# One more tile in the ring of x, and a fill, an unread write and the end marks set apart, in a fused attention and mixture-of-experts kernel

## The chip, the cores and the metric

The kernel runs on one core of a Trainium2 chip. The metric is the device time of one execution in microseconds; the time before is the median of three runs, and one further execution was profiled.

## What is computed

The reference is channel attention followed by a routed two-layer network on its output. Shapes: q, k, v are 4 x 5056 x 256, so there are 20224 tokens of 256 numbers; 8 experts with 256 x 1024 and 1024 x 256 weights.

```python
qn = q / (np.linalg.norm(q, axis=1, keepdims=True) + 1e-06)
kn = k / (np.linalg.norm(k, axis=1, keepdims=True) + 1e-06)
s = kn.transpose(0, 2, 1) @ qn / tau
a = softmax of s over its last axis
x = (v @ a).reshape(20224, 256)

do_compute = x @ w_skip > 0
out = x.copy()
xc = x[do_compute]
logits = xc @ w_gate
e_idx = np.argmax(logits, axis=1)
gate_w = softmax(logits)[row, e_idx]
for e in range(8):
    h = np.maximum(xc[e_idx == e] @ w1[e], 0.0)
    y[e_idx == e] = gate_w[e_idx == e, None] * (h @ w2[e])
out[do_compute] = xc + y
```

## The kernel before

**Stages.** Each of the four batches is cut into four chunks of ten tiles of 128 tokens, 16 chunks in all. For a chunk c, `scores` (L743) multiplies k by q into a sum over the batch, ten steps of two fp32 matmuls, each of which the profile shows as two records. `softmax` turns a batch's sum into the matrix `aug`, split in a high and a low part for exact enough products. For a chunk d, `attend` (L816 to L818) multiplies v by it, five products of twelve matmuls, each into one of the buffers `px`. `keep_x` (L825, L826) copies a product out of `px` on ScalarE (ACT): x goes into a tile `xo` of the ring `xos`, the router's logits into `lg`. `store` (L835 to L838) writes x to `out`, and `route` finds each token's place in its expert's list and scatters the chunk's ten tiles of 128 rows with indirect DMAs from GpSimd (POOL) into `srt` (L899). After every second scatter `pace` (L650) writes zeros on POOL that nobody reads.

**Experts.** The lists of the first `D0` = 6 chunks are enough to begin: seven blocks of 512 tokens of one expert are loaded ahead (`load_ahead`: the columns `xs` by L285, the rows `xg` by L289), multiplied (`first_ahead`, `second_ahead`, L338 to L340 and L361 to L365), finished on VectorE (DVE, L371) and scattered into `out` (L236). When all lists stand, `end_lists` (L671) writes marks behind each list on POOL, four indirect DMAs from the tile `none`, so that reads past an end find no token. `no_rows` (L644) fills 1024 rows behind the last list from the same tile. After the marks come eight small tiles (`Small`, rows `yg` by L530 to L532, weights `v1r` and `v2r` by L248), between the last blocks ahead, and then a loop over large halves.

**What sets the order.** All of this up to the loop is written as tasks of a planner, `Plan`: each task has an engine (D is the queue of SyncE, SP, which issues nearly all loads and stores, in order), a cost, dependencies and a due time. `PLACES` gives due times to PE's steps: A are scores, B are products with v, H blocks ahead, S small tiles. The planner runs its tasks by their costs and writes the instructions in the order that results; on each engine that order is then fixed, and each instruction waits for what it needs. A task `t` of chunk `d` that takes a tile of the ring gets the dependencies `stored[d - NXO]` and `sorted_[d - NXO]`.

**Waits between DMAs on one tensor.** All scatters, marks and loads touch `srt`, at addresses known only at run time. Helpers name groups of accesses that need not wait for each other: `in_list` puts scatters and marks into the group "scatter"; `beside(i, group, others)` puts an instruction into `group` and frees it from those of `others`. Loads ahead are put into "first lists" and freed from "later lists", and scatters of chunks from `D0` on into "later lists" and freed from "first lists". The marks are in neither.

Of the kernel before, what the change touches and what calls it, by code (L numbers as in the profile page):

```python
# [20 lines left out]
P = 128  # L21
B = 4
N = 5056
C = 256
# [11 lines left out]
S1 = 120  # L36
# [9 lines left out]
NA = 266  # L46
JH = J // 2
NQ = 5
NXO = 3

PLACES = """
A0 -212.84 779.51, A1 1321.85 2287.98, A2 1288.02 1918.41, A3 921.83 1283.14, A4 -211.85 1066.57, A5 1.96 1135.44, A6 1521.56 1748.04, A7 866.77 2427.61, 
A8 1669.19 1909.96, A9 1529.84 1745.34, A10 49.51 1125.18, A11 964.56 1241.96, A12 76.13 775.39, A13 1533.28 1646.93, A14 284.14 322.32, A15 605.99 1645.34, 
B0 -553.38 1624.65, B1 1059.41 1229.58, B2 1324.08 2043.89, B3 774.09 2431.92, B4 187.89 1016.60, B5 1367.03 1932.84, B6 157.71 569.73, B7 202.72 464.71, 
B8 855.77 2530.12, B9 1438.10 1858.11, B10 1153.34 1832.22, B11 1096.41 1886.67, B12 777.75 2410.50, B13 798.41 1410.74, B14 1275.11 2037.27, B15 1124.02 1912.70, 
H0 756.73 1449.91, H1 1567.64 1958.30, H2 211.59 521.38, H3 380.89 734.47, H4 1225.45 2144.35, H5 297.48 436.13, H6 1041.42 1976.08, S0 1664.16 1808.51, 
S1 1589.25 1784.53, S2 1183.50 2100.39, S3 491.56 743.28, S4 317.74 323.84, S5 1044.45 2181.99, S6 1496.20 1816.03, S7 1625.43 1829.53
"""


class Plan:
# [6 lines left out]
    def add(self, engine, cost, f=None, deps=(), due=1e9, hold=None, wait=0.0):  # L68


        ways = list(zip(engine, cost)) if isinstance(cost, tuple) else [(engine, cost)]
        t = SimpleNamespace(ways=ways, engine=ways[0][0], cost=ways[0][1], f=f, deps=[d for d in deps if d], due=due, asked=None, hold=hold, wait=wait, users=None, end=None)
        self.tasks.append(t)
        return t
# [102 lines left out]
def attn_moe(ctx: ExitStack, tc: tile.TileContext, q_k, vt, tau, w_skip, w_gate, w1, w1q, w2, out):  # L177
    nc = tc.nc
# [464 lines left out]
        to = srt[E * CAP : E * CAP + 8 * P, :].rearrange("(r p) w -> p r w", p=P)  # L643
        beside(nc.sync.dma_start(to, none.rearrange("p (o w) -> p o w", o=1).to_broadcast([P, 8, RW])), "no rows", "scatter")  # L644

    idle = none[:, :C].bitcast(mybir.dt.bfloat16)

    def pace():

# [2 lines left out]
    def in_list(i):  # L652
        for g in ("scatter", "no rows"):
            tc.declare_no_dep(i.ins, group=g, reason="no place is used twice")
        tc.add_to_no_dep_group("scatter", i.ins)

    def end_lists():
        low = tab.tile([P, 1], F32, name="low")
        V.tensor_scalar(low, pidx, float(R), None, ALU.is_ge)
        ends = tab.tile([P, E // 2], F32, name="ends")  # L660
        pairs = base.rearrange("p (k h) -> p k h", h=2)
        V.tensor_tensor(ends, pairs[:, :, 1], pairs[:, :, 0], ALU.subtract)
        V.tensor_scalar(ends, ends, float(-R), None, ALU.add)
        V.scalar_tensor_tensor(ends, ends, low, pairs[:, :, 0], ALU.mult, ALU.add)
        endi = tab.tile([P, E // 2], I32, name="endi")
        V.tensor_scalar(ends, ends, pidx, None, ALU.add)
        yield
        G.tensor_copy(endi, ends)
        yield
        for k in range(E // 2):  # L670
            i = G.indirect_dma_start(  # L671
                out=srt, out_offset=IndirectOffsetOnAxis(ap=endi[:, k : k + 1], axis=0), in_=none, in_offset=None,
                bounds_check=E * CAP - 1, oob_is_err=False)
            in_list(i)
            if k % 2:
                yield

# [317 lines left out]
    for c in range(NC):  # L995
        b, ch = divmod(c, NCH)
        ld, users = {}, ([], [])
        for h in range(2):
            cuts = {(0, 0): (0, 1, 2, 3, 4, JH), (0, 1): (0, 2, JH), (1, 0): (0, 2, JH)}.get((c, h), (0, JH))
            for j0, j1 in zip(cuts, cuts[1:]):  # L1000
                t = then("qk", add("D", 0.68 * (j1 - j0), lambda c=c, h=h, j0=j0, j1=j1: load_qk(c, h, j0, j1), due=1e9 if c else -99, hold=("part", 99) if j0 else ("qk", NQ)))
                t.users = [] if j0 else users[h]
                ld.update((h * JH + j, t) for j in range(j0, j1))
        for n in range(2):
            for h in range(2):
                begins = ch == 0 and h == 0
                s0 = then(("sq", n), add("S", 1.18, lambda c=c, n=n, h=h: squares(c, n, h), [ld[j] for j in range(h * JH, (h + 1) * JH)], hold=None if begins else ("sqh", 3)))
                users[h].append(s0)
                if begins:
                    if b:  # L1010
                        s0.deps.append(ready_a[b - 1, "n"])
                    summed[n] = s0
                else:
                    summed[n] = add("V", 1.41, lambda c=c, n=n, h=h: add_squares(c, n, h), [s0, summed[n]])
                    s0.users = [summed[n]]
            if ch == NCH - 1:
                summed[n] = add("V", 1.53, lambda n=n: fold_squares(n), [summed[n]])
        g = scores(c)
        for j in range(J):
            deps = [ld[j]]  # L1020
            if j == 0 and ch == 0 and b > 1:
                deps.append(freed_s[b - 2])
            t = then("A", add("T", 0.865, lambda g=g: next(g), deps, at("A", c, j)))
            if j % JH == JH - 1:
                users[j // JH].append(t)
        last_a = t
        if c == 2:
            third = t
        if ch == NCH - 1:
            g = softmax(b)  # L1030
            s0, = chain(g, ("S", 0.5), deps=[t])
            n0, = chain(g, ("T", 0.8), deps=[s0, summed[0], summed[1]])
            s = chain(g, ("V", 0.36), ("S", 1.65), ("V", 2.3), ("V", 1.55), ("S", 2.35), ("V", 0.35), ("S", 0.75), deps=[n0])
            m0, = chain(g, ("T", 0.45), deps=s[-1:])
            m1, = chain(g, ("S", 0.5), deps=[m0])
            m2, = chain(g, ("T", 0.9), deps=[m1])
            m3, = chain(g, ("V", 0.12), deps=[m2])
            aH, = chain(g, ("S", 0.55), deps=[m3])
            aL, = chain(g, ("V", 0.65), deps=[aH])
            m0.hold = m2.hold = ("m", 1)  # L1040
            m0.users, m2.users = [m1], [m3]
            freed_s[b], ready_a[b], ready_a[b, "n"] = s0, aL, n0
            if b:
                s0.deps.append(ready_a[b - 1])
            norms_read = s[0]
# [4 lines left out]


    routed, based, stored, sorted_ = {}, {}, {}, {}
    padded = add("D", 2.6, no_rows, [third], wait=8.0)
    for d in range(NC):
        b, ch = divmod(d, NCH)
        sv = []
# [18 lines left out]
                sv[0][0].users = [t]  # L1075
        sv[1][0].users = [t]
        stored[d] = then("st", add("D", 3.4, lambda d=d: store(d), [s], at("B", d, 4, by=16.5)))
        g = route(d)
        r = chain(g, ("V", 0.43), deps=[s] + ([routed[d - 1]] if d else []))
        r += chain(g, ("S", 0.17), ("V", 1.02), ("V", 0.33), ("S", 0.18), deps=r)  # L1080
# [106 lines left out]
    t = based[NC - 1]  # L1187
# [106 lines left out]
```

## Time and profile before

| | |
|---|---|
| median of 3 runs | 754.59 us (752.77 to 755.32) |
| the profiled execution | 751.94 us |
| its span | 750.1 us, 13405 instructions |
| PE, VectorE, ACT, POOL busy | 733.9, 504.1, 351.7, 328.6 us |
| DMA over the span | 165.99 MB, mean 221 GB/s |

The span runs from the first instruction of the profile to the last; the execution's own time has about 1.8 us around it. PE stands for TensorE, DVE for VectorE. "Idle before, releaser" in a row is the time for which the engine stood before that instruction, and what ended it; a wait for several things is put down to the one that came last by the profile, and where that had long been done it was another.

### The profile page before, as it was taken

The numbers are of one execution on the slowest core, as the hardware profiler recorded it, in microseconds if no ns is written. First come the engines' busy times: TensorE is split into PE (matmuls) and PEld (weight loads), VectorE is DVE, ScalarE is ACT, GpSimd is POOL, SyncE is SP. The second block draws the span as 40 slices with busy tenths as digits, with TensorE's granted clock in tenths as the row PEclk, the third lists the DMA queues.
The fourth block names the chain that finished last, engine by engine and source line by source line (L and its number), as shares of the span: only waits on it lengthen the run. The fifth ranks groups of instructions, "written<-read, shape, count | busy, mean of one in ns | idle before, by whom it ended". The sixth has DMA issues, their size and how long they took to land. (4 is left out here: it accounts for less than half of the span.)

```text
span 750.1 us, 13405 instructions
## 1 busy us (share of the span) xinstructions
PE 733.9 (98%) x4352; PEld 638.6 (85%) x4352; DVE 504.1 (67%) x971; ACT 351.7 (47%) x629; POOL 328.6 (44%) x370
## 2 busy tenths in 40 slices
PE   9999999999999999999998999999999999999996
PEld 7879999999999898998885777888888888888885
DVE  3878958967996887567945225456666585666665
ACT  4678748749856744451223223323334342343422
POOL 2000788888888887788452321221121222111122
PEclk9999999999999999999999999999999999999998
DMA  8998999999949587544679993342526344152531
GB/s 319 410 384 333 378 396 295 360 345 406 359 154 316 154 215 236 156 153 125 208 274 370 301 369 132 102 140 68 177 70 186 87 111 140 53 185 77 162 88 55
DMA packets 97652, 165.99 MB, mean 221 GB/s; under 512 B 50650, under 2 KB 75460, under 8 KB 89280
## 3 DMA queue, kind: packets, MB, share of 16 engines
q1 hardware_dynamic: 85136, 144.03, 57.6%
q0 software_dynamic: 11776, 21.31, 8.1%
q8 instruction: 26, 0.43, 0.2%
q14 instruction: 26, 0.21, 0.1%
q10 hardware_dynamic: 688, 0.01, 0.0%
HBM read 122.26 MB, written 53.92 MB: 235 GB/s over the span
## 5 line engine op out<-in xcount | busy, mean ns | idle before, releaser
L899 POOL DMA_INDIRECT srt<-xo,r_posi x160 | 190.9, 1193 | 115.2 <-ACT sqh L714 73.5
L236 POOL DMA_INDIRECT out<-xg x76 | 76.0, 1001 | 268.3 <-DVE xg L371 242.6
L743 PE MATMUL s<-qk 128*128 128x256 f32 x640 | 146.8, 381 | 1.6 <-DMA qk<-in_qk 1.6
L743 PEld LDWEIGHTS s<-qk 128*128 128x128 f32 x640 | 118.2, 190 | 17.9 <-DMA qk<-in_qk 3.6
L344 DVE SCALAR_TENSOR_TENSOR hL<-ph,hH 128x512 fp32r<-128x512 f32 x96 | 66.5, 692 | 59.0 <-ACT hH L343 57.9
L343 ACT ACTIVATE hH<-ph 128x512 fp32r<-128x512 f32 x96 | 57.5, 599 | 97.9 <-PE ph L340 97.9
L816 PE MATMUL px<-aH,vH 128*128 128x266 f32 x320 | 97.1, 303 | 1.5 <-ACT lg L826 1.5
L818 PE MATMUL px<-aH,vL 128*128 128x266 f32 x320 | 91.5, 286 | 0.0
L817 PE MATMUL px<-aL,vH 128*128 128x266 f32 x320 | 91.4, 286 | 0.0
L363 PE MATMUL po<-w2s,hH 128*128 128x512 f32 x336 | 83.8, 391 | 0.0
L338 PE MATMUL ph<-xH,w1H 128*128 128x512 f32 x192 | 74.9, 390 | 0.9 <-PE m L1177 0.9
L339 PE MATMUL ph<-xL,w1H 128*128 128x512 f32 x192 | 74.8, 390 | 0.0
L340 PE MATMUL ph<-xH,w1L 128*128 128x512 f32 x192 | 74.7, 389 | 0.0
L714 ACT ACTIVATE sqh<-qk 128x1280 f32<-128x1280 f32 x56 | 69.6, 1271 | 7.7 <-DMA qk<-in_qk 5.2
L825 ACT COPY xo<-px 128x512 f32<-128x512 f32 x80 | 47.1, 591 | 52.8 <-PE px L818 48.6
L363 PEld LDWEIGHTS po<-w2s,hH 128*128 128x128 f32 x336 | 61.2, 188 | 11.5
L307 ACT CAST xH<-xt 128x512 fp32r<-128x512 f32 x40 | 24.8, 624 | 89.7 <-DVE xt L305 89.4
L371 DVE SCALAR_TENSOR_TENSOR xg<-po,xg 128x256 f32<-128x256 f32 x90 | 43.5, 483 | 29.6 <-PE po L365 28.1
L816 PEld LDWEIGHTS px<-aH,vH 128*128 128x128 f32 x320 | 60.5, 189 | 2.9 <-ACT lg L826 2.0
L817 PEld LDWEIGHTS px<-aL,vH 128*128 128x128 f32 x320 | 60.7, 190 | 0.9
L818 PEld LDWEIGHTS px<-aH,vL 128*128 128x128 f32 x320 | 60.3, 188 | 0.0
L363 PE MATMUL px<-w2s,hH 128*128 128x512 f32 x216 | 57.6, 398 | 0.0
(184 smaller groups left out, 1318.3 us busy)
## 6 DMA issues: line engine op xcount, KB each, us to landing
qk<-in_qk SPq DMA_DIRECT2D x29, 1280.0 KB, 12.7
vf<-in_vt SPq DMA_DIRECT2D x32, 640.0 KB, 7.7
out<-xo SPq DMA_DIRECT2D x12, 1280.0 KB, 8.8
xg<-srt SPq DMA_DIRECT2D x20, 516.0 KB, 3.2
xs<-srt SPq DMA_DIRECT2D x80, 128.0 KB, 3.4
v1r<-in_w SPq DMA_DIRECT2D x10, 1024.0 KB, 7.2
v2r<-in_w SPq DMA_DIRECT2D x10, 1024.0 KB, 8.6
w1r<-in_w1q SPq DMA_DIRECT2D x8, 1024.0 KB, 5.6
```

What stands on the lines that cost most here:

```text
L236: i = (G.indirect_dma_start(out=out, out_offset=IndirectOffsetOnAxis(ap=ls, axis=0), in_=src, in_offset=None, bounds_check=NTOK - 1, oob_i ...
L338: T.matmul(ph, self.w1H[:, fs], self.xH[:, kb, :], start=(kb == 0), stop=False)
L339: T.matmul(ph, self.w1H[:, fs], self.xL[:, kb, :], start=False, stop=False)
L340: T.matmul(ph, self.w1L[:, fs], self.xH[:, kb, :], start=False, stop=(kb == 1))
L344: V.scalar_tensor_tensor(self.hL[:, f, :], ph, 0.0, self.hH[:, f, :], ALU.max, ALU.subtract)
L363: yield T.matmul(po, self.hH[:, f, ts], self.w2s[:, f, :, :], start=(f == 0), stop=False, skip_group_check=True)
L714: S.activation(to, qk[c, h][:, n], AF.Square)
L743: T.matmul(sums[b][:, cb, :], kt[:, j % JH, cb * P : (cb + 1) * P], qt[:, j % JH, :], start=(ch == 0 and j == 0 and cb == 0), stop=(ch == ...
L816: T.matmul(px[:, i, :NA], vH[:, kb, js], aH[:, kb, :], start=(kb == 0), stop=False)
L817: T.matmul(px[:, i, :NA], vH[:, kb, js], aL[:, kb, :], start=False, stop=False)
L818: T.matmul(px[:, i, :NA], vL[:, kb, js], aH[:, kb, :], start=False, stop=(kb == 1))
L899: i = G.indirect_dma_start(out=srt, out_offset=IndirectOffsetOnAxis(ap=posi[:, t : t + 1], axis=0), in_=xos[d][:, t, :], in_offset=None, b ...
```

## The change

The ring of x gets a fourth tile, and the space for software descriptors is set to 4096 bytes a partition. `pace` writes to a tile `idle` of its own rather than to `none`. The fill `no_rows` is due after the store of chunk 11 instead of after the third chunk of scores. The marks join "later lists" and are freed from "first lists". All places are new (the table's rows are not shown).

```diff
-NXO = 3
+NXO = 4
...
-    idle = none[:, :C].bitcast(mybir.dt.bfloat16)
+    idle = pb.tile([P, 512], mybir.dt.bfloat16, name="idle")
...
                 out=srt, out_offset=IndirectOffsetOnAxis(ap=endi[:, k : k + 1], axis=0), in_=none, in_offset=None,
                 bounds_check=E * CAP - 1, oob_is_err=False)
             in_list(i)
+            beside(i, "later lists", "first lists")
...
         last_a = t
-        if c == 2:
-            third = t
...
-    padded = add("D", 2.6, no_rows, [third], wait=8.0)
...
         stored[d] = then("st", add("D", 3.4, lambda d=d: store(d), [s], at("B", d, 4, by=16.5)))
+        if d == 11:
+            padded = add("D", 2.6, no_rows, [stored[d]], wait=8.0)
...
-    nc = bacc.Bacc("TRN2", target_bir_lowering=False, num_devices=1)
+    nc = bacc.Bacc("TRN2", target_bir_lowering=False, num_devices=1, dynamic_dma_scratch_size=4096)
```

On SP near the start, before (L688 loads q and k, L694 loads v, L644 is the fill; the names in brackets are the semaphores waited for, DMAHW of SP's DMAs, DMASW of POOL's):

```order
L688 DMA qk<-in_qk 128x2560 [waits DMAHW4_49,PE_49,Activation_49]
L694 DMA vf<-in_vt 128x1280
L644 DMA srt<-none 128x8x258 [waits Pool_49]
L694 DMA vf<-in_vt 128x1280 [waits DMAHW5_49]
L688 DMA qk<-in_qk 128x2560 [waits DMAHW6_49,PE_49,Activation_49]
```

And now, at the same place (lines are one further on), then where the fill stands now, between stores of chunk 11 and loads:

```order
L689 DMA qk<-in_qk 128x2560 [waits DMAHW4_49,PE_49,Activation_49]
L695 DMA vf<-in_vt 128x1280 x2
L689 DMA qk<-in_qk 128x2560 [waits DMAHW5_49,PE_49,Activation_49]
L695 DMA vf<-in_vt 128x1280 [waits DMAHW6_49,DMAHW1_49,DVE_49]
L689 DMA qk<-in_qk 128x2560 [waits DMAHW7_49,PE_49]
```

```order
L285 DMA xs<-srt 32x16x64 [waits DMAHW4_49]
L838 DMA out<-xo 640x1x256 [waits DMAHW5_49,Activation_49]
L839 DMA out<-xo 576x1x256 [waits DMAHW6_49]
L644 DMA srt<-none 128x8x258 [waits DMAHW3_49,DMAHW4_49,DMAHW2_49,DMAHW7_49,DMAHW1_49,Pool_49]
L695 DMA vf<-in_vt 128x1280 [waits DMAHW0_49,DVE_49,Activation_49]
L285 DMA xs<-srt 32x16x64 [waits DVE_49]
```

The fill has left the first loads and stands in the last third of the lists; there it waits for five of SP's DMAs, and a load of v and the next columns stand behind it.

On POOL at the end of the lists, before (L899 the last scatter, L671 the marks, L236 the scatter of a finished block):

```order
L899 DMA srt<-xo,r_posi 167424x258 [waits DMASW7_49]
L650 MEMSET none 128x512 [waits Pool_49]
L668 CAST endi<-ends 128x4 [waits DVE_49]
L671 DMA srt<-none,endi 167424x258 [waits DMAHW3_49,DMAHW4_49,DMAHW2_49,DMAHW5_49,DMAHW0_49,DMAHW6_49,DMASW0_49,Pool_49]
L671 DMA srt<-none,endi 167424x258 [waits DMASW1_49]
L236 DMA out<-xg_150 20224x256 [waits DMASW4_49]
```

And now:

```order
L900 DMA srt<-xo,r_posi 167424x258 [waits DMASW7_49]
L650 MEMSET idle 128x512 [waits Pool_49]
L668 CAST endi<-ends 128x4 [waits DVE_49]
L671 DMA srt<-none,endi 167424x258 [waits DMASW0_49,Pool_49]
L671 DMA srt<-none,endi 167424x258 [waits DMASW1_49]
L236 DMA out<-xg_151 20224x256 [waits DMAHW5_49,DMASW4_49]
```

The first mark waits for none of SP's DMAs any more; the order on POOL is otherwise the same there, and the block's first scatter now waits for one of them.

On PE in the last third of the scores, now (L744 scores, L874 and L875 the router's two small products, L817 to L819 products with v); before, the longest run of scores in that stretch was x18 and then, among other small products, x2, x2 and x8:

```order
L819 MATMUL px<-aH,vL 128x266
L874 MATMUL m<-r_rc,tri_r 128x8
L875 MATMUL m<-r_rc,ones 128x8
L744 MATMUL s<-qk 128x256 x36
L874 MATMUL m<-r_rc,tri_r 128x8
L875 MATMUL m<-r_rc,ones 128x8
L744 MATMUL s<-qk 128x256 x16
L817 MATMUL px<-aH,vH 128x266
```

Two rows x36 and x16 are 18 and 8 steps of scores, and no product with v stands between them.

## Rows read from the trace of the kernel before

**Rows 1.** The page: its span, and its first part (busy us, share, instructions).
```profile
span 750.1 us, 13405 instructions
...
PE 733.9 (98%) x4352; PEld 638.6 (85%) x4352; DVE 504.1 (67%) x971; ACT 351.7 (47%) x629; POOL 328.6 (44%) x370
```

**Rows 2.** Stretches of 20 us: length, busy us (instructions) by engine, clock, DMA share, GB/s.
```profile
20.00:40.00 20.00, 20.00 (x94) 17.62 (x93) 17.77 (x17) 12.88 (x11) 0.00 (x0) 1.00 1.02 388
...
380.00:400.00 20.00, 17.22 (x91) 14.45 (x90) 9.41 (x18) 3.47 (x7) 9.45 (x11) 1.00 0.86 265
...
500.00:520.00 20.00, 20.00 (x106) 17.17 (x105) 13.16 (x21) 8.10 (x14) 3.99 (x4) 1.00 0.24 70
```

**Rows 3.** Waits of PE over the span: us in total, times, longest.
```profile
PE px L338 <- DVE xg L371: 2.8, 1, 2.8
PE s L743 <- DMA qk<-in_qk: 1.6, 2, 1.1
PE px L816 <- ACT lg L826: 1.5, 1, 1.5
PE m L637 <- DVE ones L188: 1.1, 1, 1.1
...
PE px L338 <- ACT lg L826: 0.4, 1, 0.4
```

**Rows 4.** Timeline of SP's queue, start: start us, us, what.
```profile
24.31 0.43 SPq L644 DMA_DIRECT2D srt<-none  x1
```

**Rows 5.** Timeline of PE, 40 to 50 us; in brackets idle before.
```profile
46.98 3.29 PE L743 MATMUL s<-qk 128*128 128x256 f32 x14 [1.13 <-DMA qk<-in_qk]
```

**Rows 6.** DMA issues: count, KB each, median us to landing.
```profile
qk<-in_qk SPq DMA_DIRECT2D x29, 1280.0 KB, 12.7
...
srt<-none SPq DMA_DIRECT2D x1, 1032.0 KB
...
yg<-srt SPq DMA_DIRECT2D x6, 32.0 KB, 7.2
```

**Rows 7.** Timeline of all engines, 236 to 250 us.
```profile
237.88 2.14 POOL L899 DMA_INDIRECT srt<-xo,r_posi  x1 [0.30 <-issue]
...
242.34 0.27 ACT L854 ACTIVATE r_ex<-r_d 128x80 f32<-128x80 f32 x1
...
243.79 0.59 ACT L825 COPY xo<-px 128x512 f32<-128x512 f32 x1 [1.17 <-PE px L818]
...
244.50 0.39 PE L816 MATMUL px<-aH,vH 128*128 128x266 f32 x1 [1.49 <-ACT lg L826]
```

**Rows 8.** Timeline of POOL, 355 to 480 us.
```profile
362.39 1.67 POOL L899 DMA_INDIRECT srt<-xo,r_posi  x1 [0.30 <-issue]
...
374.00 0.99 POOL L671 DMA_INDIRECT srt<-none,endi  x1 [9.22 <-DMA xs<-srt]
```

**Rows 9.** Waits of SP's queue over the span: us in total, times, longest.
```profile
SPq L835 <- ACT lg L826: 35.7, 9, 9.7
...
SPq L530 <- DMA srt<-none,endi: 8.5, 1, 8.5
```

**Rows 10.** Timeline of SP's queue, 195 to 480 us.
```profile
382.15 0.55 SPq L530 DMA_DIRECT2D yg<-srt  x1
...
387.10 0.33 SPq L289 DMA_DIRECT2D xg<-srt  x1
```

**Rows 11.** Timeline of all engines, 383 to 400 us.
```profile
395.06 0.27 PE L545 MATMUL pt<-ident,yg 128*128 128x128 f32 x1
...
395.92 0.23 DVE L424 TENSOR_SCALAR xg<-xg,nobody 128x4 int32<-128x4 int32 x1 [9.80 <-DMA xg<-srt]
...
398.11 0.47 PE L338 MATMUL px<-xH,w1H 128*128 128x512 f32 x1 [2.78 <-DVE xg L371]
```

**Rows 12.** POOL's groups of instructions: count, busy us, mean ns, idle before.
```profile
L899 POOL DMA_INDIRECT srt<-xo,r_posi x160 | 190.9, 1193 | 115.2 <-ACT sqh L714 73.5 <-issue 33.0 <-ACT vH L700 4.5
```

**Rows 13.** The instructions of L899: ns min/median/max, first and last start.
```profile
L899 POOL DMA_INDIRECT srt<-xo,r_posi x160: 967/976/2294, 78.4 to 362.4; - x160
```

More of the change, by code (lines that the diff above doesn't have):

```diff
@@ L48 @@
 NQ = 5
-NXO = 3
+NXO = 4
 PLACES = """
[L52 to L57, printed above, removed]
+A0 528.48 1452.52, A1 3184.40 4408.51, A2 792.13 1023.06, A3 252.20 522.53, A4 -169.38 752.75, A5 -57.84 1453.36, A6 771.95 1071.41, A7 3565.70 3749.89,
+A8 2343.25 4858.37, A9 2676.18 4808.97, A10 -11.60 505.60, A11 2939.01 4268.88, A12 2857.30 4693.88, A13 713.29 889.88, A14 2524.70 4847.59, A15 2977.06 4231.86,
+B0 -393.53 2038.01, B1 555.93 1055.38, B2 3575.63 3974.72, B3 131.93 537.84, B4 3755.68 3848.25, B5 3068.56 4489.92, B6 3478.70 3824.72, B7 3105.49 4256.81,
+B8 286.27 1382.62, B9 42.23 360.94, B10 404.85 1018.53, B11 312.41 1350.19, B12 2787.34 4449.17, B13 137.04 1522.07, B14 3583.82 3688.63, B15 565.89 1002.33,
+H0 397.82 1232.06, H1 264.78 1379.84, H2 150.18 1626.03, H3 688.52 1010.98, H4 215.36 363.73, H5 587.46 815.24, H6 3348.65 3854.04, S0 3492.96 3788.29,
+S1 522.33 1261.58, S2 3398.52 4294.41, S3 249.74 409.48, S4 637.71 1155.54, S5 3455.28 3763.95, S6 3617.40 3646.85, S7 3070.45 4154.10
 """
```

## The prediction

> **What bounds the kernel now.** I read the page's busy times first: TensorE (PE) is busy for 733.9 of 750.1 us [rows 1]. That share alone does not say that PE is the limit, because matmul ends are modelled, so I went to the table of stretches: PE is filled in 20 to 40 us and in 500 to 520 us (20.00 of 20), and falls to 17.22 in 380 to 400 us [rows 2]. Whatever makes another engine faster is worth only what PE now waits for. The waits of PE give the whole budget: eight kinds, 8.8 us in all, of which the four that matter here are 2.8 us on DVE's xg, 1.6 us on loads of qk (two waits, the longest 1.1), 1.5 us and 0.4 us on ACT's lg [rows 3]. The first wait of the program, 1.1 us on `ones` [rows 3], is outside the change, and so is the tail after the last matmul. The change issues the same matmuls, so it can gain at most 8.8 - 1.1 = 7.7 us; it can lose without a bound. I then followed the four waits back, one by one.
>
> **Part 1, the 1 MB fill moves from 24 us to after chunk 11.** Before, SP issues the fill of the rows behind the lists at 24.31 us [rows 4]; it writes 1032 KB [rows 6]. In 20 to 40 us the DMA engines are used in full, at 388 GB/s [rows 2], so the fill costs all transfers behind it 1.057 MB / 388 GB/s = 2.7 us. PE's only wait on qk after the start is 1.13 us at 46.98 us [rows 5], in the stretch that this backlog reaches. Loads that come up to 2.7 us sooner cover 1.1 us, so I take **-1.1 us**, with bounds 0 (the load was late because its buffer came free late, and the fill is no part of it) and -1.1. Its new place has a price of its own. There the fill waits for five hardware queues, those of loads ahead, as it is not marked apart from them, and behind it on SP stand a load of v and the next columns. The columns before it are issued ahead of two stores that wait for ACT, so they have time to land; the nearest small load out of the lists landed in 7.2 us [rows 6]. I take 0, with an upper bound of 7.2 us on SP, which PE would see only if v were that late.
>
> **Part 2, four tiles of x.** The scatter of chunk d reads tile d mod 3; chunk d+3 may not be copied into it until its last scatter has landed. The place where this bites is at 240 us. GpSimd (POOL) ends the tenth scatter of chunk 8 at 237.88 + 2.14 = 240.02 us. ACT has done its exponentials at 242.34 + 0.27 = 242.61 us, and starts the first copy of chunk 11 only at 243.79 us, after 1.17 us of idle time. The view names PE, but the matmuls that it needs were long issued; what is left is the scatter's landing, 3.8 us after its end. PE's next product needs that copy's buffer, and starts 1.49 us late at 244.50 [rows 7]; the 0.4 us of [rows 3] follows 2 us later from the same copies. With four tiles chunk 11 waits for chunk 7, which is a full chunk of ten scatters earlier, so the copy starts when ACT is ready: 1.2 us sooner. That is the lower bound; 1.5 + 0.4 = 1.9 us is the upper. I take **-1.5 us**, nearest to PE's own row.
>
> **Part 3, the end marks no longer wait for loads ahead.** Before, POOL ends the last scatter at 362.39 + 1.67 = 364.06 us and then stands for 9.22 us until 374.00, for the landing of columns that were loaded ahead [rows 8]. The change takes these queues out of the wait (the order above). Three things follow this wait. SP holds 8.5 us for the marks [rows 9] before it issues the first small tile's rows at 382.15, and everything on SP stands behind that, the rows xg of the next large block among it, at 387.10 [rows 10]. DVE idles 9.80 us for these rows, until 395.92, and PE 2.78 us for DVE, until 398.11 [rows 11]. With the marks 9.2 us sooner, SP runs about 8.5 us sooner, and xg is there at about 387.4 instead of 395.9, while PE wants it some 2.8 us before 398.11, at 395.3, less what parts 1 and 2 gain (2.6): 392.7. So 5 us of cover replace the stall: **-2.8 us**. Lower bound 0, if xg then waits for the scatters of the block before; those come sooner by the same 9.2 us, so I keep the full value. Upper bound 2.8. What is late next there is the small tile: PE transposes it at 395.06 [rows 11], and such rows land 7.2 us after their issue [rows 6]; the change puts that transpose one product step earlier in PE's order, and 8.5 us of lead cover this.
>
> **Parts 4 and 5, at nothing.** The unread write moves to a tile of its own with the same 128x512 shape; only its wait for the fill's reading goes, and that had landed. The places: PE enters products 41 times from other work instead of 43 in the order, and the work is the same. The space for descriptors is set to 4 KB a partition. [...]
>
> **Sum.** 1.1 + 1.5 + 2.8 = 5.4 us. The profiled execution took 751.94 us; it becomes 746.5. The median of the runs shown is 754.59, 2.65 us over it, and I take the same saving from it: 754.6 - 5.4 = **749.2 us**. From 500 us on PE is filled [rows 2] and the loop's order is the same, so nothing later can take the saving back, nor add to it.
>
> **Rivals.**
> *The new order gives the saving back (chance 0.15).* In the change PE has 26 steps of scores with only two small products between, where before the longest such run had 15. 14 records took 3.29 us [rows 5], four make a step, so 26 steps take some 24 us and eat 26 x 256 KB = 6.8 MB: 283 GB/s, beside stores and scatters. Five half chunks are buffered; a freed one is wanted again four halves later, after 4 x 4.7 = 19 us, against 12.7 us from issue to landing [rows 6]. That leaves 6 us. SP's longest wait of a store for ACT, with loads behind it, was 9.7 us [rows 9]; 9.7 - 6 = 3.7 us of PE. Then 749.2 + 3.7 = 752.9, and with two such places 756. For it: loads of qk do stand behind stores on SP. Against: the buffers fill during the six products ahead of the run.
>
> *POOL's stage gets longer: slower (chance 0.08).* From 78.4 to 362.4 us POOL scatters almost without a pause [rows 13]. Its 160 scatters take 1193 ns in the mean [rows 12], and 967 at the least [rows 13], so (1193 - 967) x 160 = 36 us are stretch, and which DVE work stands beside a scatter is what the new places change. If the stretch doubles, the marks start at 364 + 36 = 400 us, 26 us later than before. PE's order is fixed, so it stands at the first small tile: slack 395.06 - (382.15 + 7.2) = 5.7 us, less the 2.6 us by which it arrives earlier and one step of 2.7 us, leaves 0.4. So 754.6 - 2.6 + 26 - 0.4 = 778 us. It decides at 374.00: marks after that are slower than before. For it: stretches to 2.14 us [rows 7]. Against: DVE's work is the same. [...]
>
> *Descriptors run short (chance 0.02).* If POOL had to see each scatter land, 3.8 us after its end as the copy of chunk 11 did [rows 7], up to 160 x 3.8 = 608 us would come on its stage, and the time would be over 1000 us. A scatter starts every (362.4 - 78.4) / 159 = 1.8 us [rows 13], so some three are under way at a time; it decides where fewer fit. Against: none of POOL's waits before is for its own scatters in that stage.
>
> *No effect of the marks (chance 0.1).* The wait is gone from the order, but the rows may be held by the earlier scatters or by DMA engines busier in 365 to 380. Then only parts 1 and 2 stay: 754.6 - 2.6 = 752.0.
>
> **How the numbers follow.** The forecast has 0.65, 748 to 751. A measurement of this kernel can tell about 0.3% from no change, 2.3 us here. Faster by more: the forecast, two thirds of the marks' rival and a third of the first rival, 0.65 + 0.07 + 0.05 = 0.77. Slower by more: POOL, descriptors and a small part of the first rival, 0.11. The rest, 0.12, is the same. The range begins at 746.5, which is 754.6 less the 7.7 us of budget and 0.4 for the spread of a median (the runs shown lie between 752.77 and 755.32), and ends at 754.0, where it takes in the lost marks, one stall of the new order, and leaves out the slow rivals.
>
> **What would show it.** Right: no PE wait on qk near 47 us; the first copy of each chunk follows ACT's own work; the first mark within 1 us of POOL's last scatter, near 365 us; no wait of PE on xg near 395 us; the sum of PE's waits at 3 to 4 us. Wrong: marks after 374 us, a wait on qk in the long run of scores, a mean scatter over 1.3 us, or new waits of PE above 5 us in all.

## The result, and the profile after

The changed kernel took **746.73 us** (median of 6 runs, 745.55 to 747.84); the kernel before, run beside it, 754.72 us (751.69 to 755.32). The ratio is 0.9901, 95% interval 0.9881 to 0.9921: 8.0 us faster by the medians. The profiled execution took 746.60 us, 5.34 less than that of before. So the two profiles differ by what was forecast (5.4), and the medians by half as much again. That gap is the main thing to explain.

The page after, its span and first part:

```profile
span 744.9 us, 13424 instructions
...
PE 733.3 (98%) x4352; PEld 639.9 (86%) x4352; DVE 505.7 (68%) x971; ACT 351.6 (47%) x629; POOL 329.2 (44%) x370
```

The waits of PE after (us in total, times, longest), to be held against [rows 3]:

```profile
PE m L637 <- DVE ones L188: 1.1, 1, 1.1
PE px L557 <- ACT hH L435: 1.0, 1, 1.0
PE ph L338 <- PE m L1177: 0.9, 1, 0.9
PE px L817 <- ACT lg L827: 0.8, 3, 0.4
PE m L874 <- ACT r_rc L871: 0.2, 1, 0.2
PE px L365 <- DVE hL L437: 0.2, 1, 0.2
```

They sum to 4.2 us, from 8.8, and PE is busy for 0.6 us less. 4.6 + 0.6 = 5.2 us is the whole difference of the spans, 750.1 - 744.9. The wait for qk at 46.98 us is gone. The smaller wait for qk that is gone too stands at 5.29 us in the timeline of PE before, 19 us ahead of the fill:

```profile
5.29 36.22 PE L743 MATMUL s<-qk 128*128 128x256 f32 x164 [0.43 <-DMA qk<-in_qk]
```

The second profile of the kernel before (before_again, below) does not have it either, so it is no effect of the change. Of the 1.9 us for lg, 0.2 us are left at the place of [rows 7], and 0.6 us stand between 64 and 67 us, where there was no such wait. The 2.8 us for xg have left the list, and a wait of 1.0 us at a small tile (L557) is in it; further down these turn out to be one wait.

The stretches of 20 us after (length, busy us by engine, PE's clock, DMA share, GB/s):

```profile
40.00:60.00 20.00, 20.00 (x102) 17.59 (x101) 17.87 (x20) 19.01 (x23) 0.00 (x0) 1.00 0.96 386
200.00:220.00 20.00, 20.00 (x106) 18.00 (x105) 18.93 (x28) 9.52 (x13) 17.65 (x16) 1.00 0.59 232
380.00:400.00 20.00, 18.99 (x98) 14.74 (x97) 8.33 (x18) 4.24 (x8) 4.17 (x5) 1.00 0.96 304
```

PE is filled where it waited for qk, and in 200 to 220 us, where the long run of scores stands; in 380 to 400 us it has 18.99 of 20, from 17.22 [rows 2]. In the timeline of all engines after, 236 to 250 us, ACT's first copy follows its own exponentials:

```profile
240.47 0.27 ACT L855 ACTIVATE r_ex<-r_d 128x80 f32<-128x80 f32 x1
...
240.65 0.57 ACT L826 COPY xo<-px 128x512 f32<-128x512 f32 x1
```

No idle time stands before the copy, where there were 1.17 us [rows 7]. The timeline of POOL after, 350 to 400 us, has the last scatter and the first mark:

```profile
361.45 1.05 POOL L900 DMA_INDIRECT srt<-xo,r_posi  x1 [0.30 <-issue]
...
363.44 0.99 POOL L671 DMA_INDIRECT srt<-none,endi  x1 [0.28 <-POOL endi L668]
```

The mark starts 0.94 us behind the scatter's end, 10.6 us sooner than before [rows 8]. The timeline of SP's queue after, 340 to 400 us:

```profile
374.05 0.54 SPq L530 DMA_DIRECT2D yg<-srt  x1
...
378.94 0.72 SPq L289 DMA_DIRECT2D xg<-srt  x1
```

Both loads are issued 8.1 and 8.2 us sooner than in [rows 10]. The timelines of DVE, ACT and PE after, 380 to 396 us, show what became of that:

```profile
390.73 0.23 DVE L424 TENSOR_SCALAR xg<-xg,nobody 128x4 int32<-128x4 int32 x1 [8.09 <-DMA xg<-srt]
...
391.96 1.09 ACT L435 ACTIVATE hH<-px 128x512 fp32r<-128x512 f32 x2 [2.53 <-PE px L340]
...
392.88 1.94 PE L557 MATMUL px<-v1r,yT 128*64 128x512 f32 x8 [1.01 <-ACT hH L435]
```

The rows xg landed only 5.2 us sooner (390.73 against 395.92): they took 11.8 us from issue, before 8.8. With them DVE finishes products (L371) out of the buffers `px`, which PE needs again. Its first such instruction, before and then after, in the timeline of DVE:

```profile
396.05 3.74 DVE L371 SCALAR_TENSOR_TENSOR xg<-px,xg 128x256 f32<-128x256 f32 x8
```

```profile
390.87 3.73 DVE L371 SCALAR_TENSOR_TENSOR xg<-px,xg 128x256 f32<-128x256 f32 x8
```

The profile puts PE's wait at 392.88 down to ACT. But PE starts 2.0 us behind DVE's first instruction here, as it did before (398.11 behind 396.05, 2.1 us), and in marks_back below it does so again although ACT had long ended. So this is the wait for xg of the kernel before, 1.0 us in place of 2.8: it is shorter, and not gone. POOL's mean scatter is 1199 ns against 1193 [rows 12].

**A way to read every profile below.** In all of them the span is PE's busy time plus the sum of PE's waits plus 7.0 to 7.8 us. The matmuls are the same, so busy time that grows needs a cause of its own. One cause is the clock: a product L339 took 0.63 us in marks_alone at a granted clock of 0.50 (at 390.30 us), and 0.40 us in before at 1.00 (at 398.42 us). The price of the clock in a stretch is estimated here as PE's busy time there times what the granted clock lacks to 1.00. Over stretches of 2 us that gives 1.4 of the 1.5 us by which marks_back is busier than after, 1.7 of 1.8 us in three_tiles, and 1.4 of the 2.1 us by which before_again is busier than before. On the other two chips it gives about half of the growth (2.1 of 4.7 us in before_third, 3.4 of 7.1 us in after_again); what the rest is, is not shown.

| kernel | median of before beside it | span | PE busy | PE waits |
|---|---|---|---|---|
| before | 754.59 | 750.1 | 733.9 | 8.8 |
| after | 754.72 | 744.9 | 733.3 | 4.2 |
| before_again | 753.95 | 752.4 | 736.0 | 9.0 |
| marks_back | 753.95 | 748.1 | 734.8 | 6.1 |
| three_tiles | 753.95 | 749.9 | 735.1 | 7.6 |
| fill_back | 753.95 | 747.1 | 733.8 | 6.1 |
| marks_alone | 774.15 | 763.8 | 739.9 | 16.9 |
| four_tiles_alone | 774.15 | 769.2 | 743.2 | 18.8 |
| places_alone | 774.15 | 777.6 | 746.8 | 23.0 |
| old_places | 774.15 | 757.7 | 739.3 | 11.3 |
| before_third | 765.27 | 763.9 | 738.6 | 17.7 |
| after_again | 765.27 | 761.9 | 740.4 | 14.0 |
| marks_alone_2 | 765.27 | 761.7 | 739.6 | 14.4 |
| old_places_2 | 765.27 | 758.7 | 739.3 | 12.3 |

The experiments ran in three groups, each on one chip. The chips differ: before took 753.95, 774.15 and 765.27 us on them. So only ratios within a group are compared. The changed kernel itself was not run again in the first group: "over the changed kernel" there is against the 746.73 us above, beside which before took 754.72 us. Ratios leave out the few executions that took over 1.5% longer than the fastest of their kernel (one of four_tiles_alone, two of places_alone, one of after_again), while medians and ranges are of all.

### The profile page after: what moved, and what is told of

Same layout as the page of the kernel before. It is cut to its first block, busy times and chain, and to the rows that moved or that the text cites. A ratio compares the mean times of both kernels' runs of the same rounds, so it can differ in the third digit from the quotient of the medians.

```text
span 744.9 us, 13424 instructions
## 1 busy us (share of the span) xinstructions
PE 733.3 (98%) x4352; PEld 639.9 (86%) x4352; DVE 505.7 (68%) x971; ACT 351.6 (47%) x629; POOL 329.2 (44%) x370
## 5 line engine op out<-in xcount | busy, mean ns | idle before, releaser
L900 POOL DMA_INDIRECT srt<-xo,r_posi x160 | 191.9, 1199 | 112.6 <-ACT sqh L715 74.0
L236 POOL DMA_INDIRECT out<-xg x76 | 75.8, 997 | 256.3 <-DVE xg L371 232.3
L744 PE MATMUL s<-qk 128*128 128x256 f32 x640 | 145.2, 381 | 0.0
L744 PEld LDWEIGHTS s<-qk 128*128 128x128 f32 x640 | 118.9, 190 | 15.8 <-DMA qk<-in_qk 1.2
L817 PE MATMUL px<-aH,vH 128*128 128x266 f32 x320 | 97.2, 304 | 0.8 <-ACT lg L827 0.8
L819 PE MATMUL px<-aH,vL 128*128 128x266 f32 x320 | 91.4, 286 | 0.0
L363 PE MATMUL po<-w2s,hH 128*128 128x512 f32 x336 | 83.8, 392 | 0.0
L338 PE MATMUL ph<-xH,w1H 128*128 128x512 f32 x192 | 75.0, 391 | 0.9 <-PE m L1177 0.9
L339 PE MATMUL ph<-xL,w1H 128*128 128x512 f32 x192 | 74.9, 390 | 0.0
L340 PE MATMUL ph<-xH,w1L 128*128 128x512 f32 x192 | 74.7, 389 | 0.0
L363 PEld LDWEIGHTS po<-w2s,hH 128*128 128x128 f32 x336 | 61.2, 189 | 11.4
L371 DVE SCALAR_TENSOR_TENSOR xg<-po,xg 128x256 f32<-128x256 f32 x90 | 43.5, 483 | 29.6 <-PE po L365 28.1
L817 PEld LDWEIGHTS px<-aH,vH 128*128 128x128 f32 x320 | 60.5, 189 | 2.1 <-ACT lg L827 1.4
L819 PEld LDWEIGHTS px<-aH,vL 128*128 128x128 f32 x320 | 60.3, 189 | 0.0
L363 PE MATMUL px<-w2s,hH 128*128 128x512 f32 x216 | 57.4, 397 | 0.0
```

Of the source, the lines that this page charges most:

```text
L236: i = (G.indirect_dma_start(out=out, out_offset=IndirectOffsetOnAxis(ap=ls, axis=0), in_=src, in_offset=None, bounds_check=NTOK - 1, oob_i ...
L338: T.matmul(ph, self.w1H[:, fs], self.xH[:, kb, :], start=(kb == 0), stop=False)
L339: T.matmul(ph, self.w1H[:, fs], self.xL[:, kb, :], start=False, stop=False)
L340: T.matmul(ph, self.w1L[:, fs], self.xH[:, kb, :], start=False, stop=(kb == 1))
L363: yield T.matmul(po, self.hH[:, f, ts], self.w2s[:, f, :, :], start=(f == 0), stop=False, skip_group_check=True)
L744: T.matmul(sums[b][:, cb, :], kt[:, j % JH, cb * P : (cb + 1) * P], qt[:, j % JH, :], start=(ch == 0 and j == 0 and cb == 0), stop=(ch == ...
```

## The experiments

### First group: one part taken back

**The marks wait again.** The changed kernel without the new line; the order on every engine stays.

```diff
-            beside(i, "later lists", "first lists")
```

> The changed kernel with one thing undone: the end marks wait again for the loads ahead. The instructions stand in the changed kernel's order. My theory (the wait for loads ahead is worth 2.8 us): the first mark stands 6 to 10 us after POOL's last scatter, SP holds over 6 us for the marks, PE waits again on xg or on the first small tile for 2 to 3 us more than in the changed kernel, and the time is 746.7 + 2.8 = 749.5 us. Rival (the places do it: in the new order PE is covered at this stage): the marks are late, but PE's waits grow by under 0.5 us and the time stays at 746 to 747.5 us.

Measured: 750.16 us (12 runs, 748.03 to 755.57), ratio 0.9958 (0.9938 to 0.9978), 3.4 us over the changed kernel. The first mark waits for 7.0 us again, until 370.06, and SP holds 8.6 us for the marks. PE's largest wait is 3.1 us at L557. The timelines of ACT, DVE and PE, 388 to 396 us:

```profile
391.82 1.08 ACT L435 ACTIVATE hH<-px 128x512 fp32r<-128x512 f32 x2 [2.53 <-PE px L340]
...
392.77 3.21 DVE L371 SCALAR_TENSOR_TENSOR xg<-px,xg 128x256 f32<-128x256 f32 x7
...
394.79 1.97 PE L557 MATMUL px<-v1r,yT 128*64 128x512 f32 x4 [3.06 <-issue]
```

ACT ends at 392.90, and PE starts 1.9 us later, 2.0 us behind DVE's first product with xg. So it is DVE and xg that PE waits for here. The stretches of 2 us around it, in the columns of the 20 us above:

```profile
392.00:394.00 2.00, 0.00 (x0) 0.00 (x0) 1.33 (x4) 0.91 (x2) 0.00 (x0) 1.00 1.47 191
394.00:396.00 2.00, 1.21 (x4) 0.58 (x6) 1.92 (x5) 0.00 (x0) 1.65 (x2) 0.58 1.05 345
396.00:398.00 2.00, 2.00 (x6) 0.26 (x2) 1.68 (x3) 0.00 (x0) 1.39 (x3) 0.56 0.99 378
```

The wait at the small tile is 3.1 us in place of 1.0, and behind it PE runs at a granted clock of 0.58 and 0.56. PE is busy for 1.5 us longer than after. 10 of the 12 runs stand at a mean granted clock of 0.993 to 0.996; the two at 0.999 took 748.03 and 748.43 us. So in the new order the marks are worth the wait and, in most runs, a stretch at the lower clock on top of it.

**Three tiles.** The changed kernel with its own order, planned for four, and a ring of three.

```diff
-        xos[d] = pb.tile([P, J, RW], F32, name="xo", bufs=NXO)
+        xos[d] = pb.tile([P, J, RW], F32, name="xo", bufs=3)
```

> The changed kernel with three buffers for the tiles of x, while the planner still plans with four, so that every engine's order stays the same and only the waits at run time differ. My theory (the ring is worth 1.5 us): PE waits once or more for the copies of chunks near 225 to 245 us, 1.2 to 1.9 us in all more than in the changed kernel, and the time is about 748.2 us. A stronger form of it: in this order, which was planned for four, more chunks meet the ring, PE waits 4 us or more and the time is over 750.5 us. Rival (the stall belonged to the old order's table loads on ACT, not to the ring): no new wait, 746 to 747.5 us.

Measured: 752.36 us (12 runs, 750.9 to 754.14), ratio 0.9985 (0.9969 to 1.0002), 5.6 us over the changed kernel. PE's largest waits:

```profile
PE px L817 <- ACT lg L827: 5.2, 4, 4.4
```

The timeline of ACT at the longest of them:

```profile
189.40 0.59 ACT L826 COPY xo<-px 128x512 f32<-128x512 f32 x1 [5.42 <-DMA srt<-xo,r_posi]
```

The stretches of 2 us there:

```profile
188.00:190.00 2.00, 0.00 (x0) 0.00 (x0) 0.40 (x1) 0.60 (x3) 1.83 (x3) 1.00 1.00 422
190.00:192.00 2.00, 1.89 (x9) 1.89 (x10) 0.02 (x1) 1.95 (x5) 1.70 (x2) 0.59 0.99 370
```

ACT's copy waits 5.42 us for a scatter out of the tile that it wants. That is the mechanism of part 2, this time named by the profile itself, and at another place (189 us, where before it was 244). An order that counts on four tiles loses more without the fourth (5.6 us) than the old order stood for its ring (1.9 us).

**The fill early again.**

```diff
+        if c == 2:
+            third = t
...
+    padded = add("D", 2.6, no_rows, [third], wait=8.0)
...
-        if d == 11:
-            padded = add("D", 2.6, no_rows, [stored[d]], wait=8.0)
```

> The changed kernel with the 1 MB fill back among the first loads, after the third chunk of scores; the planner moves some steps before 130 us with it. My theory (the fill costs the loads behind it 2.7 us and PE 1.1 us): PE waits on qk again near 47 us, about 1 us, and the time is about 747.8 us. Rival (the wait near 47 us came from a buffer that was freed late): no wait on qk, and the time stays at 746 to 747.5 us.

Measured: 748.73 us (6 runs, 747.32 to 749.07), ratio 0.9934 (0.991 to 0.9958), 2.0 us over the changed kernel. PE's largest wait:

```profile
PE s L744 <- DMA qk<-in_qk: 1.7, 2, 1.4
```

The wait for qk near 47 us is back, 1.4 us where it was 1.1; the other 0.3 us stand at 5.20 us, ahead of the fill. The fill is worth 2.0 us in the medians; what it costs beside the 1.4 us of wait was not traced.

**The kernel before, once more.**

> The kernel before once more, for a second profile. Its first profile was of an execution of 751.9 us, while the median of its runs is 754.7; the changed kernel's profile was of 746.6, at its median. Theory one (the waits of the old kernel vary from run to run): in an execution near 754.7 PE's waits sum to about 11.5 us instead of 8.8, with the additional 2.8 us at the marks, the ring or the first loads. Theory two (the difference is outside PE's waits: matmul pace or the ends): the waits again sum to 8.8 us, give or take 0.5, whatever the time.

Measured: 754.26 us, 2.3 more than its first profile. PE waits 9.0 us instead of 8.8, but is busy for 736.0 us instead of 733.9. Two-microsecond stretches of this second profile:

```profile
396.00:398.00 2.00, 0.00 (x0) 0.00 (x0) 1.28 (x4) 0.60 (x2) 0.00 (x0) 1.00 1.45 187
398.00:400.00 2.00, 1.12 (x3) 0.97 (x4) 1.93 (x5) 0.00 (x0) 1.60 (x2) 0.67 1.02 306
400.00:402.00 2.00, 2.00 (x7) 1.54 (x6) 1.71 (x4) 0.00 (x0) 1.39 (x3) 0.50 1.01 384
```

And of the first profile, on which the prediction stood:

```profile
396.00:398.00 2.00, 0.00 (x0) 0.00 (x0) 1.93 (x6) 0.62 (x2) 0.67 (x1) 1.00 1.47 210
398.00:400.00 2.00, 1.89 (x8) 1.61 (x9) 1.93 (x5) 0.00 (x0) 1.39 (x3) 1.00 0.93 381
400.00:402.00 2.00, 2.00 (x11) 0.98 (x11) 0.99 (x2) 0.82 (x2) 1.70 (x2) 1.00 1.01 383
```

The wait for xg was 3.6 us in the second and 2.8 in the first. Behind the longer one the granted clock was 0.67 and 0.50 until about 402 us; behind the shorter one it kept 1.00. The clock falls right behind a stretch with 0.00 of 2 us of PE, but the first profile has such a stretch too and kept 1.00. By the rows the drop costs about 1.4 us (an estimate: 1.12 x 0.33 + 2.00 x 0.50). The two busy times differ by 2.1 us, of which 0.4 lie in the first 8 us, where the first profile has its wait of 0.43 us instead.

The 23 runs of before beside this group say that the first profile was among the better ones: the 7 at a mean granted clock of 0.997 or more took 752.2 us in the mean, the 7 at 0.993 or less 755.1. This mean holds the time behind the last matmul too, where the granted clock is 0.50 in the first profile (746 us to the end; the mean is 0.997 in that profile, without a drop on the way, and 0.996 in the second, with one), so it tells the two kinds apart only roughly; 15 of the 23 stand below 0.996. All 6 runs of the changed kernel stand at 0.998 or 0.999.

### Second group: one part alone, on a chip where before took 774.15 us

**The marks alone**, in the kernel before, whose order stays:

```diff
+            beside(i, "later lists", "first lists")
```

> The kernel before with part 3 alone: the end marks are set apart from the loads ahead; the order on every engine stays that of the kernel before, with its ring of three, its fill and its places. My theory now (wait and clock): the change takes away the wait for xg near 395 us (2.8 us in the first profile of before, 3.6 us in the second) and with it the stretch at a granted clock of 0.50 behind it, which cost 1.7 us in the second profile. So 754.0 - (2.8 to 3.6) - 1.7 = 748.7 to 749.5 us at the median, all runs at a mean granted clock of 0.997 or more, and runs nearer together than those of before (750.6 to 756.0). First rival (the wait alone, the clock has another cause): 754.0 - 2.8 = 751.2 us, with runs at 0.993 still among them. Second rival (the mark needs the new order): no change, 753 to 755 us.

Measured: 765.96 us (6 runs), ratio 0.9885 (0.9843 to 0.9927). The gain is larger than either theory gave. PE's largest wait has the name of the one that was to go, and another place. The timeline of PE at the place of [rows 11], where 2.78 us stood before:

```profile
411.60 0.27 PE L545 MATMUL pt<-ident,yg 128*128 128x128 f32 x1
411.62 0.47 PE L338 MATMUL px<-xH,w1H 128*128 128x512 f32 x1
```

No wait is left there. The largest wait stands 101 matmuls earlier in PE's order, ahead of an earlier block's products. All engines, 376 to 395 us:

```profile
388.59 1.00 DVE L371 SCALAR_TENSOR_TENSOR xg<-px,xg 128x256 f32<-128x256 f32 x2 [6.18 <-remote]
388.77 2.06 ACT L435 ACTIVATE hH<-px 128x512 fp32r<-128x512 f32 x4 [11.67 <-remote]
...
389.74 0.76 PE L338 MATMUL px<-xH,w1H 128*128 128x512 f32 x1 [5.12 <-DVE xg L371]
```

"remote" is the view's word for a release that no record of this core stands for; DVE and ACT go on together. The mark does not wait for loads any more: it starts at 372.52, and what it waits for is POOL's own instruction, as after. SP issues its next loads late too (v1r at 384.89, v2r only at 388.51; the same pair stood 1.2 us apart in before_again). So the wait that the theory names is gone, but a longer one of another cause stands ahead of it, with a stretch at a granted clock of 0.50 behind it, and what the clock gives back is not shown. The medians say that the marks' line alone is worth about 1% on this chip; no profile of before was taken on it, so where that 1% comes from stays open.

**The ring and the descriptors' space alone**, in the kernel before, whose order stays:

```diff
-        xos[d] = pb.tile([P, J, RW], F32, name="xo", bufs=NXO)
+        xos[d] = pb.tile([P, J, RW], F32, name="xo", bufs=4)
...
-    nc = bacc.Bacc("TRN2", target_bir_lowering=False, num_devices=1)
+    nc = bacc.Bacc("TRN2", target_bir_lowering=False, num_devices=1, dynamic_dma_scratch_size=4096)
```

> The kernel before with the ring of four x tiles and the 4 KB space for descriptors alone; the order on every engine stays that of the kernel before, which is planned for three. Theory: the copies of chunk 11 no longer wait for chunk 8's scatter, so the waits for lg of 1.5 and 0.4 us go: 752.1 to 752.5 us at the median, and the wait for xg near 395 us and the spread of the runs stay. Rival (the ring matters only in an order planned for it, since another engine is as late): 753.5 to 754.5 us. Second rival (the small space for descriptors holds POOL up): a mean scatter over 1.3 us and a time over 756 us.

Measured: 771.15 us (12 runs), ratio 0.9969 (0.994 to 0.9998). 0.31% of 754 us is 2.3 us, a little above the 1.5 to 1.9 of the first theory, but its interval reaches from nothing to twice that and holds the rival too, and the profile does not show the theory's reason. At the place of [rows 7] PE still waits 2.12 us for lg (at 248.62). ACT copies chunk 11 at 247.93 right behind its exponentials (247.75), and with three tiles it does so as well on the third chip (before_third, 246.50 behind 246.33): ACT itself is late there, which is what the rival says. The mean scatter is 1164 ns, and 1163 in marks_alone on the same chip, so the space of 4096 bytes for descriptors costs POOL nothing that shows.

**The new places alone.** The edit is the table `PLACES`, whose rows are not shown; the next one puts the old table into the changed kernel.

> The kernel before with the new table of places alone, planned for three x tiles, with the fill and the marks as before. Theory: the places are worth nothing by themselves, 753 to 755 us, with the wait for xg near 395 us still there. Rival (the places carry part of the gain): 747 to 751 us. Second rival (the places suit only a ring of four, and cost with a ring of three): 755 us or more, with waits of PE for lg over 3 us in all.

Measured: 779.8 us (12 runs), ratio 1.0081 (1.0046 to 1.0116): slower. PE waits longest for the router's r_rc, 5.2 us in four times. The new places carry no gain; put on the old kernel they cost 0.8%. The waits for lg are 2.0 us, not over 3 as the second rival had it, so its reason (the ring) is not shown.

**The old places in the changed kernel.**

> The changed kernel with the table of places of the kernel before: ring of four, fill after chunk 11, marks apart, 4 KB for descriptors, idle tile. Theory: these parts carry the gain by themselves, 746.5 to 748.5 us. Rival (the new places carry 2 us or more of it): 749 to 752 us.

Measured: 764.28 us (5 runs), ratio 0.9873 (0.9843 to 0.9904). The other parts gain 1.3% here without the new places; the change itself was not run on this chip, so how much the new places would add on it is not shown.

### Third group: the change itself on a third chip

The four kernels of this group are ones shown above, without further edits: the changed kernel, the marks alone, the old places, and before.

> The changed kernel once more, beside the two others of this group, so that all stand on one chip. Chips differ (the kernel before took 754 us on one and 774 us on another), so the numbers are ratios to the kernel before on the same chip. Theory (wait and clock): the ratio stays at 0.987 to 0.992, the marks stand within 3 us behind the last scatter, and there is no wait of PE of 3 us or more and so no stretch near a granted clock of 0.50. Rival (the gain depends on the chip): over 0.994 or under 0.985.

Measured: 762.78 us (12 runs, 760.31 to 774.86) against 765.27 of before; ratio 0.9965 (0.994 to 0.999). The rival held: **the gain depends on the chip**, here 0.35% where it had been 1%. The largest waits of PE in before_third:

```profile
PE px L338 <- DVE xg L371: 4.8, 1, 4.8
...
PE s L743 <- DMA qk<-in_qk: 1.8, 2, 1.5
```

And in after_again:

```profile
PE px L365 <- DVE hL L437: 2.9, 4, 1.6
...
PE px L338 <- DVE xg L371: 1.4, 1, 1.4
```

For qk and xg the change does here what it did on the first chip: the 1.8 us for qk are gone, and so are the 4.8 us for xg. The timeline of PE, 403 to 410 us, of before_third, and behind it the same two matmuls of after_again:

```profile
404.54 0.27 PE L545 MATMUL pt<-ident,yg 128*128 128x128 f32 x1
409.58 0.76 PE L338 MATMUL px<-xH,w1H 128*128 128x512 f32 x1 [4.78 <-DVE xg L371]
```

```profile
406.53 0.27 PE L545 MATMUL pt<-ident,yg 128*128 128x128 f32 x1
406.55 0.48 PE L338 MATMUL px<-xH,w1H 128*128 128x512 f32 x1
```

The 1.4 us for xg in the list of after_again stand at 389.65, ahead of the earlier block where marks_alone has its 5.1 us. But the wait for hL grows (2.0 in before_third), one of 1.5 us for r_rc is new, and PE's busy time is 1.8 us longer than in before_third. Stretches of 2 us of after_again show a part of that:

```profile
368.00:370.00 2.00, 1.33 (x8) 0.99 (x6) 1.97 (x2) 1.07 (x2) 1.81 (x1) 1.00 0.38 58
370.00:372.00 2.00, 0.86 (x4) 0.60 (x4) 2.00 (x5) 0.01 (x1) 1.64 (x3) 1.00 0.70 262
372.00:374.00 2.00, 1.96 (x7) 1.35 (x6) 1.90 (x7) 0.00 (x0) 1.55 (x2) 0.55 1.02 419
374.00:376.00 2.00, 2.00 (x7) 1.59 (x6) 1.90 (x4) 0.00 (x0) 1.70 (x2) 0.60 0.97 406
```

No single wait of PE in this profile is over 1.9 us, and still the clock falls to 0.55; it falls a second time at 184 to 188 us (0.61 and 0.53). My expectation that it would stay up without a wait of 3 us fell: here it fell behind stretches in which PE had 1.33 and 0.86 of 2 us.

> The kernel before with the marks set apart, once more. Theory (wait and clock): on a chip where the marks follow the last scatter and their rows come in the usual 4 to 6 us, the wait for xg near 395 us goes, and with it the half clock behind it: a ratio of 0.992 to 0.995. Rival (the wait alone, 2.8 us of 754): 0.996 to 0.997. Second rival, after the first run of this kernel (0.9885, with a wait for xg of 5.1 us left in it): the marks' waiting costs more in the median run than any profile of before shows, 0.986 to 0.990.

Measured: 761.81 us (12 runs), ratio 0.9956 (0.9927 to 0.9984). The interval holds both the theory and its rival. A wait of 4.7 us for xg is listed, as in the first run of this kernel, and as there it stands ahead of the earlier block (at 386.99, behind a stand of DVE of 5.87 us put down to "remote"). At the place where before_third stood for 4.78 us, L338 follows L545 at once (409.03 behind 409.00). So the wait that hangs on the marks went on this chip too, and another took its place. SP is late by itself: it issues yg at 386.11, 12.0 us behind the last mark (4.7 us in before_again), and its rows have no wait for the marks there.

> The changed kernel with the places of the kernel before, beside the changed kernel itself on this chip. Theory: the new places are worth nothing by themselves, so the time stands within 1.5 us of the changed kernel's. Rival (the new places lose or win, as the 0.8% that they cost alone suggests): 2 us or more to one side.

Measured: 762.64 us (12 runs), ratio 0.9965 (0.9944 to 0.9987), 0.14 us from the changed kernel. On this chip the new places are worth nothing that shows, as forecast.

> The kernel before, unchanged, for a third profile of it. Theory: PE waits 2.8 us or more for xg near 395 us; if that wait is over 3 us, a stretch at a granted clock of 0.50 follows it and the execution is 2 us or more above 751.9 us (on the first chip's scale); if it is 2.8 us or less, the clock stays at 1.00. Rival: the drop comes without regard to the wait.

Measured: 765.61 us. The wait for xg is 4.8 us, until 409.58, and the stretches of 2 us around its end stand at a granted clock of 0.50:

```profile
408.00:410.00 2.00, 0.41 (x1) 0.45 (x2) 1.89 (x6) 0.00 (x0) 0.97 (x1) 0.50 1.16 285
410.00:412.00 2.00, 2.00 (x6) 1.52 (x6) 1.97 (x5) 0.00 (x0) 1.62 (x2) 0.50 0.96 373
```

## Why the prediction was right, and where its sizes were off

The sign and the mechanisms of all three parts came out on the first chip. The time did not come out well: 746.73 us is 2.5 us under the 749.2 forecast, outside the 748 to 751 that had most of the chance, and 0.2 us inside the lower end of the range.

- **The ceiling did not hold.** "It can gain at most 8.8 - 1.1 = 7.7 us" took PE's waits for the whole budget. The gain was 7.9 us from the median of 754.59, and 8.0 us beside its own runs of before. PE's busy time is no constant of the matmuls: it was 2.7 us longer in before_again than after. That the range held is owed to the 0.4 us that it added for the spread of a median, and so to luck.
- **Part 1, the fill: 1.1 forecast, 1.1 measured.** The wait at 46.98 us went, and 1.4 us came back there with the fill. The other wait for qk in [rows 3] stands at 5.29 us and has nothing to do with it. No wait for v or qk shows at the new place of the fill.
- **Part 2, the ring: 1.5 forecast, 1.1 in the profile.** The waits for lg fell from 1.9 to 0.2 us at the ring's place, and 0.6 us of them are new at 64 to 67 us. Taking the tile away from the new order costs 5.6 us, but that is a price of the new order, not the gain over the old one. The fourth tile alone gave 0.31% on another chip, with the wait still there.
- **Part 3, the marks: 2.8 forecast, 1.8 in the profiles.** The wait for xg went from 2.8 to 1.0 us. The step "xg is there at about 387.4" was wrong by 3.3 us, since it took the landing time of before (8.8 us), and it was 11.8. The "5 us of cover" were also counted to the landing of xg, while PE waits for DVE's products with it, 2 us later. So the sign "no wait of PE on xg near 395 us" did not come out: PE was ready at 391.87 and stood for 1.0 us. In 380 to 400 us the DMA engines moved 304 GB/s against 265 [rows 2]; whether that is why xg took longer is not shown.
- **The step that failed** is "I take the same saving from it". The profiled execution of before lay 2.65 us under its median, and I carried that difference over as if it belonged to every kernel. The changed kernel's profile lies 0.13 us under its median. 5.34 of the two profiles and 2.65 - 0.13 of the gap make 7.9, which is the difference of 754.59 and 746.73. Against the second profile of before, of an execution at its median, the changed kernel has 4.8 us less of waits and 2.7 us less of busy time, about half of it the stretch at the lower clock behind the wait for xg. By their mean clocks most executions of before have such a stretch and none of the changed kernel has; at which place is shown for the profiled ones alone.
- **Parts 4 and 5, at nothing.** Right as far as it was tried: the old places in the changed kernel give the same time on the third chip. On the first chip they were not tried. The new places are not nothing by themselves (places_alone). The unread write, and the space for descriptors without the ring, were not tried alone.
- **The rivals.** The long run of scores did not starve: PE has 20.00 of 20 us there, and no wait on qk is left. POOL's stage was not longer, 1199 ns a scatter, marks at 363.44. The long scatters do stand beside DVE's work: in the profile of before, the 40 of 1.2 us or more have L705 or L718 beside them for 1.14 us in the mean, the 101 under 1.0 us for 0.07 us; after, 41 have 1.10 us and 99 have 0.06 us of the same two (there L706 and L719). Descriptors did not run short in any way that shows: of POOL's waits at L900 none is put down to a scatter, and the mean of 1199 ns is that of before within 6 ns. How many scatters the space of 4096 bytes holds is shown by no run. That the marks have no effect is refuted by marks_back.

The sums of single parts do not add up to the whole: taken back one at a time they cost 3.4, 5.6 and 2.0 us, 11.0 together, where the change gave 8.0. For the ring this was to be expected, since the new order is planned for four tiles; for the others it is not shown why.

**Open:** why the gain is 1.0% on one chip and 0.35% on another. The waits that remain on the third chip show in orders old and new. ACT has waits that are put down to "remote" in marks_alone on the second chip (11.7 us in one) and in after_again on the third (8.4 us in six), and none in before and after on the first chip; what releases them is in no record.

## What to carry to other kernels

Split every span into PE's busy time and PE's waits: where the matmuls are the same and busy time grows, look for stretches at a lower granted clock, and work out how much of the growth they explain. Compare waits by their place in the engine's order, not by the name of their releaser: one wait had three names here (xg, hH, issue), and two waits had one. One profile is one execution: if its time differs from the median, ask what the median run has that it has not, before a saving is carried from one to the other. Give a wait that is removed its price with the clock behind it, and measure the change on more than one chip before a figure of 1% is quoted.

## What was not expected of the hardware

- A wait of PE of 3.1 to 5.1 us was followed by a stretch at a granted clock of 0.50 to 0.67 in marks_back, three_tiles, before_again, marks_alone, before_third and marks_alone_2; one of 2.8 us in the first profile of before was not. The length of the wait alone does not tell: in old_places PE waits 2.0 us at the most, and the profiled run still stands at a mean granted clock of 0.994, where the first profile of before, without a drop on the way, has 0.997; in after_again shorter waits in a row had the same effect.
- Chips differ in one stage of this program. Up to 166 us the changed kernel's records of ACT on the third chip agree with the first profile within 0.25 us. Then ACT's second copy out of `px`, at 166.74 us on the first chip, starts at 167.75 on the third, 1.04 us of it idle. From there on the third chip adds waits, 9.8 us of them by the table, and 7.1 us of busy time. None of that is in the loop's products L338 to L340 into `ph` and L363 into `po` (308.2 us there, 308.4 on the first chip), and from 500 to 700 us PE is filled on both (200.00 of 200).
